# Last attention unit in two query halves, output groups gathered ahead, masked query copies on GpSimd, query tiles 40 rows earlier

## The chip, the cores and the metric

The kernel runs on one core of one Trainium2 chip. The metric is the time of one execution on the device in microseconds (us), as the median of several executions. A profiled execution shows a *span* some 1.7 us shorter, because the span runs only from the first to the last instruction (797.01 us and a span of 795.3 us for the kernel before). Every execution also has a mean granted clock of TensorE, where 1.0 is full speed.

## The reference, cut to what matters

```python
def reference(A_x, A_wqkv, A_wo, B_x, B_w1, B_w3, B_w2):   # x: 1 x 2048 x 512, bf16; 32 heads of 16
    def _A_ref(x, wqkv, wo):
        q, k, v = ...                                       # x @ wqkv, split in heads
        scores = jnp.einsum("bhqd,bhkd->bhqk", q, k) * (Dh ** -0.5)
        p = _softmax(scores, axis=-1)
        o = jnp.einsum("bhqk,bhkd->bhqd", p, v)
        return ... @ wo
    def _B_ref(x, w1, w3, w2):                              # F = 1792
        return (_silu(x @ w1) * (x @ w3)) @ w2
    xn = _layernorm(A_x, axis=-1)
    return A_x + _A_ref(xn, A_wqkv, A_wo) + _B_ref(xn, B_w1, B_w3, B_w2)
```

The work is 2048 x 2048 scores for each of 32 heads. Their exponentials are nearly all that ScalarE does (747.6 of its 772.0 busy us in the kernel before).

## The kernel before

When the kernel is built, a greedy plan in Python lays every instruction in order on its engine, by modelled durations. So a change in one place shifts instructions everywhere.

The attention is 32 *units*: 4 chunks of 512 queries times 8 groups of 4 heads. A unit has 32 *blocks* of scores (128 x 1024), so there are 1024 blocks. ScalarE takes the exponential of most blocks in one instruction. VectorE takes the rest: one instruction reads the scores from PSUM, and four further passes over two blocks at a time run in SBUF. Projections, the feed-forward part and the output projection fill TensorE between the scores.

A pair of units needs a query tile. It is projected by TensorE, scaled by VectorE, and copied twice under a mask (even heads, odd heads):

```python
def tile_QT(qc, i):
    ...
    def emit():
        q = P.op("dve", lambda e: e.tensor_scalar(QT[:, s1, :], bank(bk), QS, None, ALU.mult), ...)
        rel(q)
        q = P.op("dve", lambda e: e.tensor_scalar(QT[:, s0, :], QT[:, s1, :], msk[:, 0:1], None, ALU.mult), ..., lock=True)
        done[("QTm", u0)] = q.end + _LAT
        q = P.op("dve", lambda e: e.tensor_scalar(QT[:, s1, :], QT[:, s1, :], msk[:, 1:2], None, ALU.mult), ..., lock=True)
        done[("QTm", u0 + 1)] = q.end + _LAT
```

A query tile may start once the plan has come to within 60 rows of its unit (a row is half a block, and a unit has RPU = 64 rows). I call this distance the *lead*:

```python
for qc in range(NQC):
    for i in range(NG // 2):
        if qc + i > 0:
            crit.append((max(1, (qc * NG + 2 * i) * RPU - 60), k, tile_QT(qc, i)))
```

The last unit ends in a chain of its own. It copies the products out of PSUM, sums the columns, takes reciprocals, spreads them over the partitions and normalises, all for 512 queries at once:

```python
def last_end(o):
    def copy():      # ACT: U <- PV, 512 columns
    def col_sums():  # PE: 4 matmuls against sell
    def inv():       # DVE: reciprocal; a copy of the sums; l_check (three small operations for the check flag)
    def spread():    # PE: 16 matmuls of the reciprocals against the identity
    def norm_b():    # DVE: onorm <- U * mask * spread; releases ("ON", qc, "B")
```

The last four row tiles of the output add up in a PSUM bank: 14 feed-forward groups of 4 matmuls, and then, in the tail, 5 groups with `wo`:

```python
ats = [og(g, (qc * NP + g) % NON, ("ON", qc, g)) for g in range(NP)]
last_b = [og(NP - 1, ON_B, ("ON", qc, "B"))]
...
gr = {2: ats + last_b, 3: ffn, 4: ats, 5: ffn + res + ats + last_b}[part]
```

Parts 3 and 2 make three of the last row tiles: part 3 goes to SBUF ahead, and part 2 is added to it in the tail. Part 5 is the fourth row tile, made as one sum that stays in its bank.

Of the kernel before, what the change touches and what calls it, by code (L numbers as in the profile page):

```python
# [144 lines left out]
_LAT = 0.06  # L145
# [892 lines left out]
def _plan_fast(nc, ps, flag, A_x, A_wqkv, A_wo, B_w1, B_w3, B_w2, out):  # L1038
# [15 lines left out]
    NR = NU * RPU  # L1054
    NPR = 12
# [12 lines left out]
    D_STOP = 6  # L1068
    NW = 3
    PVQ = 28  # L1070
    R_LAG = 2.5
    A_SOON = 0.7
# [16 lines left out]
    with ctx:  # L1089
# [338 lines left out]

        def tile_KT(i, sc):
# [16 lines left out]
        def tile_QT(qc, i):  # L1446
# [9 lines left out]
            def evac(bk, o, rel):  # L1456
                def emit():
                    q = P.op("dve", lambda e: e.tensor_scalar(QT[:, s1, :], bank(bk), QS, None, ALU.mult),  # L1458
                             reads=[("ps", bk)], writes=[("QT", s1)], dur=d_cost(512), name="evQ")
                    rel(q)  # L1460
                    q = P.op("dve", lambda e: e.tensor_scalar(QT[:, s0, :], QT[:, s1, :], msk[:, 0:1], None, ALU.mult),
                             reads=[("QT", s1), ("msk", 0)], writes=[("QT", s0)], dur=s_cost(512), name="evQ", lock=True)
                    done[("QTm", u0)] = q.end + _LAT
                    q = P.op("dve", lambda e: e.tensor_scalar(QT[:, s1, :], QT[:, s1, :], msk[:, 1:2], None, ALU.mult),
                             reads=[("QT", s1), ("msk", 1)], writes=[("QT", s1)], dur=s_cost(512), name="evQ", lock=True)
                    done[("QTm", u0 + 1)] = q.end + _LAT
                P.post("dve", emit, ready=o.end + _LAT, prio=1)
# [109 lines left out]

        def late():
            return left[NU - 1] <= D_STOP and st["hold_d"] == 0 and pbuf[2] <= P.t or st["pos"] >= NR
        ON_B = (NQC * NP) % NON  # L1580

        def tile_OUT(tg, part):
# [9 lines left out]
            last_b = [og(NP - 1, ON_B, ("ON", qc, "B"))]  # L1592
            res = [(lambda i: ident[:, 32 * i:32 * i + 32], xr[:, ts % 2, :], [("ident",), ("xr", ts % 2)],
                    lambda: have(("xl", tg)))]
            gr = {2: ats + last_b, 3: ffn, 4: ats, 5: ffn + res + ats + last_b}[part]
# [39 lines left out]
            def cond():  # L1635
                if part == 4:
                    return have(("OSUM", tg), ("ON", qc, NP - 1))
                if part == 2:
                    return have(("OSUM", tg)) and (st["pos"] >= NR or late())
                if part == 5 and tg == NT - 1 and not late():  # L1640
                    return False
# [6 lines left out]
                return have(("ON", qc, NP - 1))  # L1648
# [45 lines left out]
        for qc in range(NQC):  # L1694
            for i in range(NG // 2):
                if qc + i > 0:
                    crit.append((max(1, (qc * NG + 2 * i) * RPU - 60), k, tile_QT(qc, i)))
# [35 lines left out]
        taken = [[False] * (RPU // 2) for u in range(NU)]  # L1733
        left = [RPU // 2] * NU
        st["ua"] = 0

        def a_next(avoid=None):
            while st["ua"] < NU and left[st["ua"]] == 0:
                st["ua"] += 1
            if st["ua"] >= NU:  # L1740
# [3 lines left out]
            if avoid is not None and i % 2 == avoid:  # L1744
                for k in range(i + 1, min(i + 6, RPU // 2)):
# [4 lines left out]
        def d_next():  # L1750
# [4 lines left out]
            if left[u] <= D_LEFT and u + 1 < NU:  # L1755
                u += 1
            elif u == NU - 1 and left[u] <= D_STOP:
                return None
            c = [i for i in range(RPU // 2) if not taken[u][i]][:2]
# [8 lines left out]
        def score(b0, name, u, ix):  # L1768
            kt, j0 = ix // 2, ix % 2 * 2
            r0 = u * RPU + 2 * ix  # L1770
            g = u % NG
            g = g // 2
            if not have(("QTm", u), ("KTm", g, kt // 4)):
                return None
            rd = [("QT", u % 4), ("KT", g, kt // 4)]
            mms = []
            for i in range(2):
                j = j0 + i
                mms.append((b0 + i, KT[32 * j:32 * j + 32, g, kt * 128:(kt + 1) * 128],
                            QT[32 * j:32 * j + 32, u % 4, :], 32 * j))  # L1780

            def f(e, mms=tuple(mms)):
                for (b, l_, r_, rp) in mms:
                    ins = e.matmul(bank(b), l_, r_, start=True, stop=True, tile_position=(rp, 0))  # L1784
# [12 lines left out]
        def open_bufs():  # L1797
# [3 lines left out]
            if not st["early"] and idle((4, 5)):  # L1801
# [83 lines left out]
        def try_d():  # L1885
# [19 lines left out]
            if sl is None:  # L1905
                sl = dcur[0] = {"y": None, "p1": 0, "n": 0, "ch": [], "done": 0, "max": 2 if u < NU - 1 or left[u] > D_ONE else 1}
# [95 lines left out]
        def try_pv():  # L2002
            u = pv_unit[0]
            if u >= NU:
# [5 lines left out]
            vi = int(u % NG >= 2)  # L2010
            oldest = P.t
            for j in range(4):
                for tk in tasks[u][j]:
                    if tk[0] <= P.t and have(("V", tk[1], vi)):
# [5 lines left out]
            closed = left[u] == 0 and sum(ntask[u]) == 64 + 4 * nd_unit[u]  # L2020
            if len(pick) < 4 and not closed and P.t - oldest < 2:
                return False
            g = u % NG
            mms, rd, rels = [], [], []
            for j in sorted(pick):
# [4 lines left out]
                stop = left[u] == 0 and npv[u][j] == NT + 2 * ndj[u][j]  # L2030
                w_ = Vaug[:, tk[1], 4 * (g // 2) + j, 0:17] if g % 2 == 0 else Vaug[:, tk[1], 4 * (g // 2) + j, 1:33]
                mms.append((j, w_, tk[2], start, stop))
                rd += [("V", tk[1], vi), tk[3]]
                rels.append(tk[4])

            def f(e, mms=tuple(mms)):
                for (j, v_, p_, s0, s1) in mms:
                    ins = e.matmul(bank(PV)[32 * j:32 * j + (17 if g % 2 == 0 else 32), :], v_, p_, start=s0, stop=s1, tile_position=(0, 32 * j))  # L2038
# [4 lines left out]
            if left[u] == 0 and not any(tasks[u]) and st["n_exp"] >= 0 and \  # L2043
                    sum(ntask[u]) == 64 + 4 * nd_unit[u] and npv[u] == ntask[u]:
# [5 lines left out]
        def unit_end(u, o):  # L2050
            h = u % 2
            qc, pi = divmod(u // 2, NP)
            UK = [("Uc",)] + [("Uo", j_) for j_ in range(4)] if h == 0 else [("Ut",)]
# [40 lines left out]
            def beside_p1():  # L2094
                return st["p1_at"] == P.t

# [21 lines left out]
            if u == NU - 1:  # L2118
                return last_end(o)
            P.post("dve", e0, ready=o.end + _LAT, prio=0, cond=lambda: u < 2 or h == 1 or ("e5", u // 2 - 1) in done)  # L2120

        def last_end(o):
            u = NU - 1
            qc = NQC - 1

            def copy():
                q = P.op("act", lambda e: e.activation(U[:, 1, :], bank(PV), ACTF.Identity), reads=[("ps", PV)],
# [243 lines left out]
```

## Time and profile before

| | before |
|---|---|
| median (range) | 798.34 us (797.80 to 800.65, 4 executions) |
| blocks on ScalarE / VectorE | 798 / 226 |
| last exponential ends | 782.32 us |
| last addition ends (the *tail* is from the last exponential to here) | 790.80 us, so 8.48 us of tail |
| from there to the end (output transfer) | 4.48 us |
| mean TensorE clock of the profiled execution | .996 |

Two groups of the page tell how the exponentials are shared. The columns are line, engine, operation, output and input with their sizes and count; then the total busy us and the mean ns of one; then the idle time ahead of them and what ended most of it:

```profile
L1847 ACT ACTIVATE f_PT<-ps 128x1024 bf16<-128x1024 f32 x798 | 747.6, 1138 | 4.4 <-PE ps L1784 3.7
L1920 DVE TENSOR_SCALAR f_xd<-ps 128x1024 int16<-128x1024 f32 x226 | 275.1, 1217 | 3.0 <-PE ps L1784 2.7
```

ScalarE waits only 4.4 us in all ahead of its 798 blocks. To end sooner it needs fewer blocks, or fewer of these waits, or a shorter tail after the last block.

### The profile page before, as it was taken

How to read it: one execution, taken by the hardware profiler on the slowest of the kernel's cores; microseconds unless marked ns; L12 is line 12 of the kernel's file. 1: busy time of each engine (PE TensorE's matmuls, PEld its weight loads, DVE VectorE, ACT ScalarE, POOL GpSimd, SP SyncE). 2: the span in 40 equal slices, each digit the busy share in tenths (PEclk: the TensorE clock that was granted, in tenths of full speed). 3: DMA queues.
4: the chain of work that ended last, by engine and by line, in shares of the span. 5: the costliest groups of instructions: out<-in, count | busy, mean ns of one | idle time of the engine just before them, and what ended most of it. 6: DMA issues, size and time to landing. Idle time of an engine off the chain costs nothing.

```text
span 795.3 us, 21182 instructions
## 1 busy us (share of the span) xinstructions
PE 750.3 (94%) x9169; PEld 227.6 (29%) x9169; DVE 768.8 (97%) x1039; ACT 772.0 (97%) x872; POOL 38.0 (5%) x60
## 2 busy tenths in 40 slices
PE   8999999999899999999999999998999998999997
PEld 6332222222222222222222222222222222222223
DVE  8899999999999999999999999999999999999993
ACT  5999999999999999999999999999999999999994
POOL 3100201000010000000000000000100000000000
PEclk9999999999999999999999999999999999999989
DMA  7024033331322222233311234322223341332221
GB/s 213 2 23 118 5 35 42 36 34 36 48 35 30 30 36 48 34 48 53 45 17 15 37 47 59 49 33 45 28 22 36 54 60 22 51 35 23 22 15 33
DMA packets 83568, 32.91 MB, mean 41 GB/s; under 512 B 72073, under 2 KB 79753, under 8 KB 83465
## 3 DMA queue, kind: packets, MB, share of 16 engines
q1 hardware_dynamic: 83464, 31.46, 27.6%
q8 instruction: 74, 1.21, 0.6%
q14 instruction: 30, 0.24, 0.1%
HBM read 22.81 MB, written 2.10 MB: 31 GB/s over the span
## 4 chain that ended last, share of the span: by engine, by line
ACT 63%; DVE 23%; PE 12%; issue 1%; DVEq 0%; ACTq 0%
ACT f_PT L1847 60%; DVE f_xd L1920 8%; PE ps L1330 4%; DVE f_xd L1969 4%; PE ps L1784 4%; PE ps L2038 3%; DVE f_xd L1962 2%; ACT f_th L1544 2%; DVE f_xd L1978 2%; DVE f_xd L1984 2%; DVE f_hT L1558 2%; DVE f_t L1548 1%; PE ps L1217 1%; DVE f_U L2056 1%; DVE f_QT L1458 0%
## 5 line engine op out<-in xcount | busy, mean ns | idle before, releaser
L1847 ACT ACTIVATE f_PT<-ps 128x1024 bf16<-128x1024 f32 x798 | 747.6, 1138 | 4.4 <-PE ps L1784 3.7
L1784 PE MATMUL ps<-f_QT,f_KT 32*128 32x512 bf16 x2048 | 310.8, 386 | 26.6 <-ACT f_PT L1847 20.4
L1920 DVE TENSOR_SCALAR f_xd<-ps 128x1024 int16<-128x1024 f32 x226 | 275.1, 1217 | 3.0 <-PE ps L1784 2.7
L2038 PE MATMUL ps<-f_PT,f_Vaug 128*17 128x512 bf16 (+1 forms) x1596 | 210.0, 386 | 3.4 <-DVE f_U L2056 2.2
L2038 PE MATMUL ps<-f_xd,f_Vaug 128*32 128x512 bf16 (+1 forms) x1356 | 182.3, 385 | 3.9 <-DVE f_xd L1969 1.6
L1784 PEld LDWEIGHTS ps<-f_QT,f_KT 32*128 32x128 bf16 x2048 | 79.6, 91 | 323.0 <-ACT f_PT L1847 259.8
L1330 PE MATMUL ps<-f_xnT,f_w 128*32 128x512 bf16 x1792 | 139.9, 384 | 3.0 <-DVE f_t L1548 1.2
L1969 DVE TENSOR_TENSOR f_xd<-f_xd 128x2048 bf16<-128x2048 bf16 x113 | 137.3, 1215 | 0.0
L1962 DVE TENSOR_SCALAR f_xd<-f_xd 128x2048 int16<-128x2048 int16 x113 | 80.5, 713 | 2.7 <-PE ps L2038 1.9
L1984 DVE TENSOR_SCALAR f_xd<-f_xd 128x2048 int16<-128x2048 int16 x113 | 78.0, 690 | 0.0
L1978 DVE TENSOR_SCALAR f_xd<-f_xd 128x2048 int16<-128x2048 int16 x113 | 77.6, 687 | 0.0
L1330 PE MATMUL ps<-f_w,f_hT 128*32 128x512 bf16 x896 | 73.0, 383 | 0.2
L2038 PEld LDWEIGHTS ps<-f_PT,f_Vaug 128*17 128x17 bf16 (+1 forms) x1596 | 51.0, 92 | 63.7 <-issue 45.8
L2038 PEld LDWEIGHTS ps<-f_xd,f_Vaug 128*32 128x32 bf16 (+1 forms) x1356 | 44.5, 92 | 51.3 <-issue 26.9
L2100 POOL TENSOR_TENSOR f_onorm<-f_U,f_R 128x256 bf16<-128x256 f32 x30 | 25.1, 842 | 703.2 <-DMA f_R<-f_Rrow 414.0
L1330 PEld LDWEIGHTS ps<-f_xnT,f_w 128*32 128x32 bf16 x1792 | 36.8, 94 | 62.2 <-issue 51.5
L1544 ACT ACTIVATE f_th<-ps 128x512 f32<-128x512 f32 x56 | 41.0, 733 | 0.0
L1558 DVE SCALAR_TENSOR_TENSOR f_hT<-f_t,ps 128x512 bf16<-128x512 bf16 x56 | 38.0, 679 | 0.4 <-PE ps L1330 0.2
L1548 DVE SCALAR_TENSOR_TENSOR f_t<-f_th,ps 128x512 bf16<-128x512 f32 x56 | 38.0, 678 | 0.3 <-ACT f_th L1544 0.3
L1330 PEld LDWEIGHTS ps<-f_w,f_hT 128*32 128x32 bf16 x896 | 19.3, 95 | 23.7 <-issue 16.3
L2056 DVE COPY f_U<-ps 128x512 f32<-128x512 f32 x31 | 21.2, 685 | 0.4 <-PE ps L2038 0.4
L1330 PE MATMUL ps<-f_wo,f_onorm 128*32 128x512 bf16 x272 | 19.9, 382 | 0.2 <-DVE f_QT L1458 0.2
(81 smaller groups left out, 240.1 us busy)
## 6 DMA issues: line engine op xcount, KB each, us to landing
f_w<-in_B_w_dram SPq DMA_DIRECT2D x112, 128.0 KB, 3.9
f_R<-f_Rrow SPq DMA_DIRECT2D x124, 32.0 KB, 4.1
f_xr<-in_A_x_dram SPq DMA_DIRECT2D x16, 128.0 KB, 2.6
f_U<-f_U SPq DMA_DIRECT2D x60, 32.0 KB, 1.9
f_w<-in_B_w_dram SPq DMA_DIRECT2D x7, 256.0 KB
f_xd<-in_A_x_dram SPq DMA_DIRECT2D x3, 512.0 KB
out_dram<-f_xn_sb SPq DMA_DIRECT2D x12, 128.0 KB
f_xd<-in_A_x_dram SPq DMA_DIRECT2D x2, 256.0 KB
```

The source lines that it names most:

```text
L1330: ins = e.matmul(bank(bk)[32 * i:32 * i + 32, 0:ncols], make_lhsT(i), rhs_ap, start=start, stop=stop, tile_position=(0, 32 * i))
L1544: q = P.op("act", lambda e: e.activation(th[:, ss, :], bank(bk), ACTF.Tanh, scale=0.5), reads=[("ps", bk)], writes=[("th", ss)], dur=a_cos ...
L1548: q2 = P.op("dve", lambda e: e.scalar_tensor_tensor(t1[:, ss, :], th[:, ss, :], 1.0, bank(bk), ALU.add, ALU.mult), reads=[("th", ss), ("ps ...
L1558: q = P.op("dve", lambda e: e.scalar_tensor_tensor(hT[:, fc, :], t1[:, ss, :], 0.5, bank(bk), ALU.mult, ALU.mult), reads=[("t1", ss), ("ps ...
L1784: ins = e.matmul(bank(b), l_, r_, start=True, stop=True, tile_position=(rp, 0))
L1847: q = P.op("act", lambda e: e.activation(PT[:, s_, :], ps[:, b0 * 512:(b0 + 2) * 512], ACTF.Exp, scale=ASC, bias=ABIAS), reads=[("ps", b0) ...
L1920: q = P.op("dve", lambda e: e.tensor_scalar(dsl[:, ys, 1024 * c:1024 * c + 1024], ps[:, b0 * 512:b0 * 512 + 1024], YB, G_LO, ALU.add, ALU. ...
L1962: P.op("dve", lambda e: e.tensor_scalar(dsl[:, NY + m_, 0:n], y, 0x7F, 0x3F00, ALU.bitwise_and, ALU.bitwise_or), reads=YK, writes=[("ds", ...
L1969: q_ = P.op("dve", lambda e: e.tensor_tensor(t_ap.bitcast(BF16), y.bitcast(BF16), t_ap.bitcast(BF16), ALU.mult), reads=YK + [("ds", NY + m ...
L1978: q_ = P.op("dve", lambda e: e.tensor_scalar(g_ap, y, -G_LO, 0.0, ALU.add, ALU.max), reads=YK, writes=[("g", g_, k) for k in range(n // 51 ...
L1984: q_ = P.op("dve", lambda e: e.tensor_scalar(y, y, 0x7F80, None, ALU.bitwise_and), reads=YK, writes=YK, dur=s_cost(n), name="e", lock=True)
L2038: ins = e.matmul(bank(PV)[32 * j:32 * j + (17 if g % 2 == 0 else 32), :], v_, p_, start=s0, stop=s1, tile_position=(0, 32 * j))
```

## The change

The intent is to free VectorE of the masked copies, so that it takes more blocks (the query tiles then have to start 40 rows earlier), and to shorten the tail by normalising half of the last unit before the last exponential and by doing output groups early. The core of the diff (cuts are marked `...`):

```diff
-    D_STOP = 6
+    D_STOP = 4                       # VectorE takes blocks until so many are left
...
-                    q = P.op("dve", lambda e: e.tensor_scalar(QT[:, s0, :], QT[:, s1, :], msk[:, 0:1], None, ALU.mult), ..., lock=True)
-                    ...              # and the second masked copy
+                    P.post("pool", lambda: part(0), ready=q.end + _LAT, prio=1, cond=beside_p1)
+                def part(i):
+                    h, cs = i // 2, slice(256 * (i % 2), 256 * (i % 2) + 256)
+                    d_ = (s0, s1)[h]
+                    q = P.op("pool", lambda e: e.tensor_scalar(QT[:, d_, cs], QT[:, s1, cs], msk[:, h:h + 1], None, ALU.mult),
+                             ..., dur=QP_DUR, extra=[st["p1_op"]])
+                    ...
+                    if i < 3:
+                        P.post("pool", lambda: part(i + 1), ready=q.end + _LAT, prio=1, cond=beside_p1)
...
-                    crit.append((max(1, (qc * NG + 2 * i) * RPU - 60), k, tile_QT(qc, i)))
+                    crit.append((max(1, (qc * NG + 2 * i) * RPU - 100), k, tile_QT(qc, i)))
...
-            gr = {2: ats + last_b, 3: ffn, 4: ats, 5: ffn + res + ats + last_b}[part]
+            na = NP - 2 if ts < 1 else NP - 1
+            gr = {2: ats[na:] + last_b, 3: ffn + ats[:na] if qc == NQC - 1 else ffn, 4: ats,
+                  5: ffn + res + ats + last_b}[part]
...
-                if part == 5 and tg == NT - 1 and not late():
-                    return False
...                                   # scores and value products of the last unit: two key tiles x 256 queries
-        def last_end(o):
+        def last_end(o, hb):          # once for each half of the queries: 256 columns,
+            ...                       # half of the sums, reciprocals, spreading and normalising;
+            ...                       # first half copied by VectorE, second by ScalarE
```

`beside_p1` lets a GpSimd copy start only together with one of VectorE's readings of scores from PSUM.

## The prediction

> **What bounds the kernel now.** I read the busy times first, then the same by stretch of the span, then the chain that ended last, then the timeline around the two places that looked odd. The first view, engine by engine over 795.3 us:
>
> ```profile
> PE 750.3 (94%) x9169; PEld 227.6 (29%) x9169; DVE 768.8 (97%) x1039; ACT 772.0 (97%) x872; POOL 38.0 (5%) x60
> ```
>
> Three engines look full and GpSimd idle. By stretch (columns: stretch, its length, then the busy time of each engine with its instruction count, the TensorE clock, the DMA share and GB/s):
>
> ```profile
> 100.00:400.00 300.00, 285.20 (x3356) 79.92 (x3353) 298.52 (x389) 299.80 (x341) 10.82 (x12) 1.00 0.29 39
> 400.00:740.00 340.00, 323.32 (x3896) 93.17 (x3892) 336.21 (x434) 339.31 (x384) 11.09 (x14) 1.00 0.28 37
> ...
> 778.00:782.40 4.40, 4.40 (x64) 1.43 (x66) 0.31 (x1) 4.32 (x5) 0.00 (x0) 1.00 0.02 4
> 782.40:786.70 4.30, 4.30 (x85) 3.13 (x83) 0.84 (x6) 0.60 (x1) 0.00 (x0) 1.00 0.00 0
> 786.70:791.00 4.30, 3.35 (x61) 1.36 (x60) 3.00 (x6) 0.60 (x1) 0.00 (x0) 1.00 0.23 71
> 791.00:795.30 4.30, 0.00 (x0) 0.00 (x0) 0.00 (x0) 0.00 (x0) 0.00 (x0) 1.00 0.26 77
> ```
>
> There are two regimes. Up to about 782 us ScalarE is the bound (339.31 of 340) with VectorE beside it (336.21): they share the exponentials, 798 blocks of 128x1024 on ScalarE and 226 on VectorE, 1024 in all. Freeing either lets the plan move blocks across. TensorE has some 5% of idle there and waits mostly for ScalarE to release score banks. From 782.4 on, ScalarE and VectorE are nearly idle and TensorE is continuously busy: a serial tail of 13 us, of which the last 4.3 us is only the output transfer. The chain that ended last, by pieces, shows what that tail is (start, duration, what):
>
> ```profile
> 781.05 1.62 PE ps L2038 x26
> ...
> 782.89 1.08 PE ps L1330 x18
> 783.97 0.98 PE ps L2134 x8
> 784.96 0.76 PE ps L1330 x12
> 785.72 0.87 PE ps L2152 x32
> 786.60 0.11 PE ps L2232
> 786.71 3.38 PE ps L1330 x60
> 790.09 0.02 issue
> 790.11 0.69 DVE f_xn_sb L1614
> ```
>
> L2038 is probabilities times V, L2134 the column sums of the last unit and L2152 the spreading of their reciprocals, L1330 here the output projection, L1614 the last addition. The output projection needs 4 row tiles x 5 groups of 4 matmuls = 80 matmuls of f_wo, all of them after 782.8 us. So the tail is bound by TensorE's *work*, not by the latency of its hops.
>
> **What the Trainium skill says.** "SBUF — State Buffer", section "Who interferes with whom": a VectorE instruction with at most one SBUF input, outside the 2-port modes, does not contend with GpSimd, while a 2-port one fully blocks it or is blocked. The change starts each GpSimd copy beside the reading of scores from PSUM (L1920). The trace agrees so far: the GpSimd normalisations, placed by the same rule, run at a median 728 ns (min 725), one in thirty at 1813. "GPSIMD Engine Reference", section "Elementwise — side-by-side cycle accounting": about 2.6 cycles per element for two inputs and 1.8 at best for one, at 1.2 GHz. For 256 elements the first gives 555 ns; the trace's 728 leaves some 173 ns of overhead. "TensorE: Matmul & The Clock Gate", section "Back-to-back issue gap": an isolated warm gap of N/2.4 + 2.5 ns, so 216 ns for 512 columns and 109 for 256. The trace agrees for 512: 60 column-tiled matmuls, four at once, take 3.38 us, which is 225 ns per group of four; no 256-column matmul of the score loop exists in it yet.
>
> **The change, part by part.**
>
> *1. Masked query copies to GpSimd.* Fifteen times, VectorE makes two masked copies:
>
> ```profile
> 68.07 0.35 DVE L1461 TENSOR_SCALAR f_QT<-f_QT,f_msk 128x512 bf16<-128x512 bf16 x1
> ...
> 68.34 0.34 DVE L1464 TENSOR_SCALAR f_QT<-f_QT,f_msk 128x512 bf16<-128x512 bf16 x1
> ```
>
> The records overlap, so I take start-to-start times: 68.07 to 68.34 to 68.60, 0.53 us the pair, 15 x 0.53 = 8.0 us of VectorE freed. A block costs VectorE, by the same start-to-start reading of the loop, 1.13 (L1920) plus half of 1.13 + 3 x 0.60 (the passes over two blocks), 2.6 us; ScalarE needs 0.917 (36.75 us for 40). If x blocks move, ScalarE saves 0.917x and VectorE 8.0 - 2.6x; equal at x = 2.3, which is **2.1 us**. A moved block adds two further value products on TensorE (some 0.2 us a block), which its 5% of idle holds. I keep 1.8 us because the plan is greedy. GpSimd gets 60 copies of 128x256 at an estimated 384 + 173 = 557 ns (skill's 1.8 cycles plus the overhead above), inside the 1.13 us of L1920; 33 us more on an engine that has 757 free.
>
> *2. Query tiles 40 rows earlier.* Four copies now wait for four score readings, some 2.6 to 4 us apart, so a tile is ready 10 to 16 us later. The 40 rows give 40 x 0.375 = 15 us (24 us per unit of 64 rows), so it balances. It also should remove one stall:
>
> ```profile
> 69.00 3.77 ACT L1847 ACTIVATE f_PT<-ps 128x1024 bf16<-128x1024 f32 x4 [1.30 <-PE ps L1784]
> ```
>
> ScalarE sat 1.30 us because the first such query tile was copied only at 67.34 to 68.7, behind the V and K tiles in the single dense bank. From row 28 instead of 68 it would come some 30 us sooner. With VectorE idle 0.75 us at the same place: **1.0 us**.
>
> *3. Last unit in halves.* The exponentials cost the same: 16 blocks of two key tiles x 256 queries for each half instead of 32 of one x 512. Matmuls of the unit double in number at half the length; the streaming time is equal, and ScalarE paces them. The first half's copy, sums (half of 0.98), spread (half of 0.87) and its two row tiles go before the last exponential. VectorE may take blocks to 4 instead of 6 before the end; it was idle from 778.3 to the last exponential at 782.33. Two blocks later at the joint rate (0.68 us a block) is 1.35 us more of VectorE, half a block: **0.35 us**.
>
> *4. Gathering ahead.* Two groups of the first row tile and three of the next two, 8 groups x 0.225 = 1.8 us of TensorE, go into the partial sums before the tail.
>
> *The tail after the last exponential.* Before, 782.33 to 790.80 = 8.47 us. TensorE work there falls by 1.8 us (part 4), 0.93 (half of sums and spread), and the groups of the first two row tiles that find room ahead. Then the latency of the second half's hops decides. From this trace's own durations, halved where the instruction is halved: last value products 0.55; copy on ScalarE 0.38 (0.60 for 512, less 256 x 0.83 ns); to TensorE 0.36; sums 0.50; reciprocal 0.25 with its wait 0.05; spread 0.5 with 0.1; normalise 0.45 with 0.1; last group of two row tiles 0.45 with 0.15; addition 0.69. Sum 4.5 us; with some unavoidable queueing behind other matmuls 5.3. **Saving 3.1 us.** The transfer of 256 KB after it stays at 4.5 us.
>
> Sum: 1.8 + 1.0 + 0.35 + 3.1 = 6.2 us. I take off 0.8 for a plan made anew (each moved tile shifts others, and the end of the D blocks can fall badly), so 5.4 us: 798.4 - 5.4 = **793.0 us**.
>
> **Rivals.** *GpSimd blocks VectorE.* If a copy outlasts L1920, the next 2-port pass waits: 60 copies x 0.3 us would be 18 us of VectorE, 26% of it on the end (0.917 / (0.917 + 2.6)), about 4.7 us given back: near 798 us. Against it: 728 ns of a two-input operation already fits. *Late query tiles.* If the chain of four copies comes late, scores of a pair of units wait; 1 us at each of 15 pairs would give a time above 800. For it: the one-tile stall above; against it: 15 us more of lead, and no other gap of ScalarE that long behind scores in the old trace. *TensorE stays the bound of the tail.* Between 775.4 and 782.4 it is busy without a gap, so work moved ahead may only push the last scores. Then only what moved before 775 counts, some 1.8 to 2.5 us rather than 3.1: 794. *The clock falls.* Around 770 to 773.4 the granted clock is 0.50 in this trace, after a stretch of less busy TensorE; a tail with waits between hops might meet such a stretch and lose 1 to 2 us.
>
> ```profile
> 770.00:773.40 3.40, 3.40 (x24) 0.66 (x22) 3.27 (x5) 3.31 (x4) 0.00 (x0) 0.50 0.67 57
> ```
>
> **Range and chances.** All gains together with no loss come to 792.2, and a luckier plan to 790; the rivals singly give 794 to 798, and the worst of them I hold for unlikely. So 793.0, range 790.0 to 796.5. 2% is 16 us, more than the whole tail: faster 0.01, within 0.98, slower 0.01.
>
> **What would show it.** In the changed trace: L1461 and L1464 gone from VectorE and 60 GpSimd copies of 0.5 to 0.6 us; about two to three more L1920 blocks than 226 and as many fewer ScalarE blocks; no 1.3 us gap of ScalarE near 69 us; the last exponential near 779 instead of 782.33; 5 to 5.5 us from there to the last addition instead of 8.47, with waits between hops where TensorE is now continuously busy; 4.5 us of transfer unchanged. It is wrong if GpSimd copies take over 1.1 us, if ScalarE shows gaps at each pair of units, or if the last exponential does not come sooner.

## The result, and the profile after

The changed kernel takes **788.87 us** (788.16 to 789.84, 4 executions), and the kernel before 798.34 us. The ratio is .9877 (95% interval .9854 to .9900). A ratio here is the mean time of one kernel's runs over that of the other's of the same rounds, so it is not quite the ratio of the medians quoted. The gain is 9.5 us where 5.4 were predicted, and the time lies below the predicted range.

Engine by engine in the changed kernel, then its span by stretches, with the same columns as in the prediction:

```profile
PE 747.1 (95%) x9337; PEld 226.8 (29%) x9337; DVE 764.8 (97%) x1023; ACT 768.5 (98%) x870; POOL 90.7 (12%) x120
```

```profile
100.00:400.00 300.00, 285.01 (x3386) 80.50 (x3386) 296.80 (x378) 298.69 (x340) 34.72 (x40) 0.99 0.30 39
400.00:740.00 340.00, 327.43 (x3908) 92.83 (x3904) 336.08 (x426) 339.96 (x385) 38.18 (x42) 1.00 0.28 37
772.50:777.50 5.00, 5.00 (x118) 3.20 (x116) 3.08 (x9) 4.54 (x5) 0.00 (x0) 1.00 0.00 0
777.50:780.00 2.50, 2.50 (x52) 1.77 (x42) 0.28 (x1) 0.38 (x1) 0.00 (x0) 1.00 0.02 7
780.00:783.40 3.40, 2.57 (x46) 0.96 (x45) 3.14 (x11) 0.60 (x1) 0.00 (x0) 1.00 0.00 0
```

The bound of the main part is as before: ScalarE is busy in 339.96 of 340 us. In the tail the first 2.5 us are still TensorE's, but then VectorE is busy in 3.14 of 3.40 us and TensorE has gaps. The copies and the moved blocks:

```profile
L1866 ACT ACTIVATE f_PT<-ps 128x1024 bf16<-128x1024 f32 x796 | 744.7, 1151 | 3.4 <-PE ps L1803 3.2
L1939 DVE TENSOR_SCALAR f_xd<-ps 128x1024 int16<-128x1024 f32 x228 | 277.2, 1216 | 2.8 <-PE ps L1803 2.5
L1471 POOL TENSOR_SCALAR f_QT<-f_QT,f_msk 128x256 bf16<-128x256 bf16 x60 | 55.3, 922 | 270.5 <-DVE f_xd L1997 112.8
```

Two blocks went from ScalarE to VectorE. A GpSimd copy takes 922 ns, not the 557 I had estimated, and so mostly just fits within VectorE's reading of scores (1216 ns; the median copy starts .25 us after it and ends .045 us before it). From the chain that ended last in the changed kernel (start, duration, what):

```profile
776.35 1.97 PE ps L2066 x58
...
778.65 0.86 PE ps L1332 x12
779.51 0.55 PE ps L2168 x4
...
780.09 0.21 DVE f_Rc L2174
...
780.36 0.18 DVE f_th L1286
...
780.78 0.17 DVE f_accb L1290
780.96 0.59 DVE f_xn_sb L1630
781.55 0.39 DVE f_onorm L2195
...
782.17 0.61 DVE f_xn_sb L1630
```

The second half's value products (L2066) and sums (L2168) are followed in this chain by VectorE alone: the reciprocal, the three check operations (L1286 to L1290), one addition (L1630), the normalisation (L2195), and the last additions. The last exponential ends at 777.46 us and the last addition at 783.37 us, so the tail is 5.91 us instead of 8.48. The transfer takes 4.74 us instead of 4.48.

So 4.9 us of the gain come *before* the last exponential (782.32 to 777.46) and 2.6 in the tail, less .3 in the transfer: 7.2 us between these two profiled executions. The medians are 9.5 us apart, because the profiled execution of the kernel before (797.01 us) was faster than its four timed ones and that of the changed kernel the slowest of its four. My sum had 3.15 us (1.8 + 1.0 + .35) ahead of the last exponential, before the shade of .8. What filled the rest, and why do the executions differ so?

One thing stands out in the timeline of ScalarE. The 1.30 us gap at 69 us is gone: one unbroken row of 50 blocks runs across it (start, duration):

```profile
49.49 46.11 ACT L1866 ACTIVATE f_PT<-ps 128x1024 bf16<-128x1024 f32 x50
```

That was predicted, and the gap is 1.3 us; from start to start ScalarE loses 1.6 us there, because two blocks begin 2.56 us apart that otherwise begin .92 us apart. The other candidate is the clock. The four executions of the changed kernel have mean clocks of .997 to .999. The 45 executions of the kernel before average .9923, and none reaches .997.

### The profile page after: what moved, and what is told of

Read it like the earlier page. It is cut to its first block, busy times and chain, and to the rows that moved or that the text cites. A ratio compares the mean times of both kernels' runs of the same rounds, so it can differ in the third digit from the quotient of the medians.

```text
span 788.1 us, 21640 instructions
## 1 busy us (share of the span) xinstructions
PE 747.1 (95%) x9337; PEld 226.8 (29%) x9337; DVE 764.8 (97%) x1023; ACT 768.5 (98%) x870; POOL 90.7 (12%) x120
## 4 chain that ended last, share of the span: by engine, by line
ACT 82%; PE 11%; DVE 5%; issue 0%; DMA 0%; POOL 0%; DVEq 0%; ACTq 0%
ACT f_PT L1866 78%; PE ps L1332 4%; PE ps L1803 4%; ACT f_th L1555 3%; PE ps L2066 3%; DVE f_xd L1939 1%; DVE f_xd L1988 1%; DVE f_xd L2003 0%; DVE f_xd L1981 0%; DMA f_xd<-in_A_x_dram 0%; DVE f_hT L1569 0%; PE ps L1344 0%; DVE f_t L1559 0%; DVE f_stats L1256 0%; DVE f_xd L1997 0%
## 5 line engine op out<-in xcount | busy, mean ns | idle before, releaser
L1803 PE MATMUL ps<-f_QT,f_KT 32*128 32x512 bf16 (+1 forms) x2112 | 313.6, 378 | 23.3 <-ACT f_PT L1866 17.2
L1939 DVE TENSOR_SCALAR f_xd<-ps 128x1024 int16<-128x1024 f32 x228 | 277.2, 1216 | 2.8 <-PE ps L1803 2.5
L2066 PE MATMUL ps<-f_PT,f_Vaug 128*17 128x512 bf16 (+2 forms) x1640 | 205.1, 378 | 1.1 <-DVE f_U L2086 0.5
L2066 PE MATMUL ps<-f_xd,f_Vaug 128*32 128x512 bf16 (+2 forms) x1416 | 181.9, 377 | 4.6 <-DVE f_U L2086 3.1
L1332 PE MATMUL ps<-f_xnT,f_w 128*32 128x512 bf16 x1792 | 143.1, 386 | 3.7 <-DVE f_t L1559 1.6
L1988 DVE TENSOR_TENSOR f_xd<-f_xd 128x2048 bf16<-128x2048 bf16 (+1 forms) x115 | 139.7, 1215 | 0.0
L1471 POOL TENSOR_SCALAR f_QT<-f_QT,f_msk 128x256 bf16<-128x256 bf16 x60 | 55.3, 922 | 270.5 <-DVE f_xd L1997 112.8
L1981 DVE TENSOR_SCALAR f_xd<-f_xd 128x2048 int16<-128x2048 int16 (+1 forms) x115 | 78.1, 679 | 3.9 <-PE ps L2066 3.1
L2003 DVE TENSOR_SCALAR f_xd<-f_xd 128x2048 int16<-128x2048 int16 (+1 forms) x115 | 78.3, 681 | 0.0
L1997 DVE TENSOR_SCALAR f_xd<-f_xd 128x2048 int16<-128x2048 int16 (+1 forms) x115 | 78.2, 680 | 0.0
L2066 PEld LDWEIGHTS ps<-f_PT,f_Vaug 128*32 128x32 bf16 (+1 forms) x1640 | 51.3, 92 | 58.6 <-issue 45.1
L2066 PEld LDWEIGHTS ps<-f_xd,f_Vaug 128*32 128x32 bf16 (+1 forms) x1416 | 46.1, 92 | 49.0 <-issue 28.5
L1332 PE MATMUL ps<-f_wo,f_onorm 128*32 128x512 bf16 x272 | 22.1, 383 | 0.3 <-DVE f_wkv L1619 0.2
```

What stands on the lines that cost most here:

```text
L1332: ins = e.matmul(bank(bk)[32 * i:32 * i + 32, 0:ncols], make_lhsT(i), rhs_ap, start=start, stop=stop, tile_position=(0, 32 * i))
L1471: q = P.op("pool", lambda e: e.tensor_scalar(QT[:, d_, cs], QT[:, s1, cs], msk[:, h:h + 1], None, ALU.mult), reads=[("QT", s1), ("msk", h) ...
L1803: ins = e.matmul(b, l_, r_, start=True, stop=True, tile_position=(rp, 0))
L1939: q = P.op("dve", lambda e: e.tensor_scalar(dsl[:, ys, 1024 * c:1024 * c + 1024], ps[:, b0 * 512:b0 * 512 + 1024], YB, G_LO, ALU.add, ALU. ...
L1981: P.op("dve", lambda e: e.tensor_scalar(dsl[:, NY + m_, 0:n], y, 0x7F, 0x3F00, ALU.bitwise_and, ALU.bitwise_or), reads=YK, writes=[("ds", ...
L1988: q_ = P.op("dve", lambda e: e.tensor_tensor(t_ap.bitcast(BF16), y.bitcast(BF16), t_ap.bitcast(BF16), ALU.mult), reads=YK + [("ds", NY + m ...
```

## The experiments

Twelve kernels ran beside the kernel before.

**The theories.** Theory C (clock): the kernel before loses time to stretches in which TensorE runs at half speed, like the one around 770 us that stood in the prediction's own view, and the change happens to remove them. Theory W (work): the gain is what the prediction listed, with a larger size of one of the parts, that is waits and VectorE time saved, and the clock plays no part. To tell them apart I took the change to pieces, and in one kernel changed the clock alone.

**A tool for reading them.** Within one kernel the span follows the mean clock (correlation -.86 for the kernel before and -.87 for the changed one). Through all executions of all kernels, some 110, I fitted straight lines with one common slope and a level for each kernel: .44 us for each .001 of clock, with a residual of .55 us (standard deviation). The level at clock 1.0 is an estimate of a kernel's span at full speed. It is given below as *span at full clock*; to be compared only with its like. Two things limit it. The slopes of the single kernels run from .14 to .70 us. And the profiled executions also fall to half clock during the output transfer (in after_again from 784.49 us to the end, in lead_only from 788.04), when TensorE has next to nothing left to do; the mean clock counts that too. So half a microsecond between two estimates means little. A check without the line: executions with a clock of .998 or more have a mean span of 793.7 us in end_filled (4 of them; this is the plan of the kernel before, which itself has none), 791.2 in lead_only (4), 788.5 in masks_only (1) and 787.0 in the changed kernel (7).

| kernel | median, us (before on the same chip) | ratio, 95% interval | mean clock | span at full clock, est. | last exponential | tail |
|---|---|---|---|---|---|---|
| before | 798.34 | | .9923 | 793.2 | 782.32 | 8.48 |
| after | 788.87 (798.34) | .9877 [.9854, .9900] | .9979 | 786.55 | 777.46 | 5.91 |
| before_again | 797.20 (799.27) | .9979 [.9965, .9992] | as before | | 782.21 | 8.63 |
| after_again | 788.92 (799.27) | .9880 [.9861, .9898] | as after | | 776.17 | 5.91 |
| masks_only | 792.39 (799.27) | .9911 [.9895, .9928] | .9952 | 788.3 | 777.65 | 8.57 |
| tail_only | 793.72 (799.27) | .9924 [.9909, .9938] | .9966 | 790.2 | 780.32 | 8.37 |
| lead_only | 793.12 (798.42) | .9936 [.9918, .9953] | .9977 | 790.45 | 777.43 | 9.01 |
| end_filled | 795.52 (798.42) | .9966 [.9949, .9984] | .9983 | 793.3 | 781.77 | 8.47 |
| whole_gather | 791.88 (798.42) | .9920 [.9901, .9939] | .9953 | 788.3 | 777.99 | 7.71 |
| no_gather | 789.53 (798.42) | .9893 [.9874, .9913] | .9986 | 787.4 | 774.54 | 8.44 |
| first_lead | 796.81 (798.80) | .9991 [.9964, 1.0019] | .9938 | 792.9 | 780.61 | 8.64 |
| other_lead | 795.08 (798.80) | .9969 [.9951, .9986] | .9953 | 792.0 | 780.17 | 8.78 |
| copy_512 | 792.36 (798.80) | .9922 [.9908, .9936] | .9970 | 789.0 | 778.64 | 5.91 |
| late_check | 790.72 (798.10) | .9906 [.9891, .9921] | .9970 | 787.2 | 776.45 | 5.96 |

The clocks of before and after are over all their executions (45 and 9), the repeats included. All results were correct.

### before_again and after_again: the two kernels unchanged

No edit. They bound what the same kernel varies by.

> The kernel before, run again, to see how its time varies by execution and with the granted TensorE clock. Theory A (states): the profile of before that the prediction was worked from was its fastest execution (797.0 against a median of 798.3), because half-speed stretches of the clock fall at random; then the clock varies between executions from 0.995 to 0.999, the time follows it by 1 to 2 us, and a half-speed stretch is not always at 768 to 775 us. Theory B (structure): the stretch at 768 to 775 us is made by this kernel's own thin TensorE work there, and it is found again in this profile.

> The changed kernel, run again. Theory A: its half-speed stretches are as frequent as those of before, at other places, and the ratio to before is about 0.990 (the profiles' 788.1 over 795.3) once enough executions are seen. Theory B: no half-speed stretch in its last 30 us, since the last unit's two halves keep TensorE busy, and the ratio stays at 0.988 or below; the last exponential ends at 777 +- 1 us and the last addition 5.5 to 6 us after it.

The half-speed stretch of the kernel before is found again in its second profile (6.8 us from 769.5 us, against 768.0 us in the first), so it seems to belong to that plan (Theory B of the two expectations), while the clock varies from execution to execution (.986 to .996). The kernel before, run as if it were a new one, came out at .9979 of itself, with an interval that leaves out 1. Its five executions happened to have clocks of .993 to .996, its partners .986 to .996. So an interval from a few executions is too narrow here, and a difference of .2% (1.6 us) between two kernels is only to be believed together with its clocks. The changed kernel repeated within .1 us at 788.92; its one slow execution (792.22 us) is also the one with the low clock (.994; the others are at .998 or above).

### masks_only: the masked copies and the lead, without the tail's changes

The kernel before with `tile_QT` of the changed one, and the lead that goes with it (with leads of 60 to 98 rows the plan for GpSimd copies did not come to an end at build time, so the copies could not be tried without the lead; a rebuild with 60, 80, 90 and 98 failed in the same way):

```diff
-                    q = P.op("dve", ... QT[:, s0, :] ... lock=True)      # and the second copy
+                    P.post("pool", lambda: part(0), ready=q.end + _LAT, prio=1, cond=beside_p1)
...                                    # part(i) as in the change
-  crit.append((max(1, (qc * NG + 2 * i) * RPU - 60), k, tile_QT(qc, i)))
+  crit.append((max(1, (qc * NG + 2 * i) * RPU - 100), k, tile_QT(qc, i)))
```

> The kernel before with only the masked copies moved to GpSimd and the query tiles 40 rows earlier; the last unit is whole and the tail is the old one. My prediction priced these at 1.8 + 1.0 = 2.8 us: 795.5. Rival (the masks' gain was mis-sized, the tail's was right): the missing 4 us are here, so 791.5. Expected in the profile either way: 228 or 229 blocks on VectorE, copies of 922 ns, no 1.3 us gap near 69 us, tail of 8.5 us from the last exponential to the last addition.

792.39 us, so 6.9 us below its partner, where prediction parts 1 and 2 together had 2.8. The last exponential came at 777.65 us, as early as in the whole change, while the tail stayed at 8.57. So the surplus over the prediction lies in these two parts, not in the tail.

### tail_only: halves and gathering, with the masked copies on VectorE

The changed kernel with the two VectorE copies put back. The lead stayed at 100.

```diff
-                    P.post("pool", lambda: part(0), ready=q.end + _LAT, prio=1, cond=beside_p1)
+                    q = P.op("dve", ... QT[:, s0, :] ... lock=True)      # and the second copy
```

> The changed kernel with the masked copies back on VectorE (tiles still 40 rows earlier); halves, gathering and new tail kept. My prediction priced the tail with its part of the last unit at 3.1 + 0.35 us and the earlier tiles at 1.0: 794. Rival (the tail or the end of the last unit was mis-sized): 790 to 791. Expected: 226 blocks on VectorE, tail 5.9 us.

793.72 us. The tail, 8.37 us, is hardly shorter than before, although the halves and the gathering are in the kernel. TensorE's timeline says why (start, duration, what):

```profile
781.69 1.12 PE L1332 MATMUL ps<-f_w,f_hT 128*32 128x512 bf16 x14
...
784.86 2.76 PE L1332 MATMUL ps<-f_wo,f_onorm 128*32 128x512 bf16 x48
```

Here the last exponential ends at 780.32 us, and of the last row tile's 56 feed-forward matmuls 28 are still to do after it, and 48 of the 80 matmuls with `wo` as well. The changed kernel has 44 with `wo` left at that point and no feed-forward matmul. So the groups with `wo` were gathered nearly as far as there; it is the feed-forward part of the last row tile that did not find TensorE time before the end. The tail's parts thus did not shorten the tail by themselves; that the other parts make the room for them fits this, but no run shows it by itself. And since this kernel, which also has the new lead, is as fast as 793.7 us, I next took the lead alone.

### lead_only: query tiles 40 rows earlier, nothing else

```diff
-  crit.append((max(1, (qc * NG + 2 * i) * RPU - 60), k, tile_QT(qc, i)))
+  crit.append((max(1, (qc * NG + 2 * i) * RPU - 100), k, tile_QT(qc, i)))
```

> The kernel before with the query tiles 40 rows earlier and nothing else; the copies stay on VectorE. My prediction gave this 1.0 us (the 1.3 us gap of ScalarE near 69 us). Expected 797 to 798 beside 798.3 to 799.3 of before, 226 blocks on VectorE. Rival (much of what masks_only gained was the lead): 795 or less.

793.12 us: **one number in one line takes 5.3 us off**, more than half of the whole change, where the prediction had 1.0. VectorE still makes the copies, and the split of the blocks is still 798 to 226. The gap at 69 us is gone here too:

```profile
48.84 32.35 ACT L1847 ACTIVATE f_PT<-ps 128x1024 bf16<-128x1024 f32 x35
```

But the profiled execution also has no half-speed stretch ahead of the output transfer, and the mean clock is .9977 instead of .9923. At equal clock the estimate is 793.2 to 790.45, so 2.7 us; the remaining 2.6 us is put down to the clock.

### end_filled: the clock alone

The plan of the kernel before, untouched, with eight groups of four dummy matmuls put into TensorE's idle moments between 745 and 775 us of the plan. They write to a bank that is free and is overwritten later, so the result is right. Each waits for the last user of that bank, so an added dependency is the only other difference.

```diff
+        FILL = [(745, 775)]
+        ...
+        for (t0_, o_, m_), (t1_, _, n_) in zip(P.pes, P.pes[1:]):
+            ...                                           # only where TensorE idles and bank 6 is free
+            o_.fn = with_fill(o_.fn, col_groups(lambda i: w2[:, 0, 32 * i:32 * i + 32], xnT[:, 0, 0:512], 512))
```

> The kernel before, its plan unchanged, with eight dummy groups of four matmuls into an idle PSUM bank hung onto matmuls already there between 760 and 773 us; the result stays right. Theory (thin TensorE work halves the clock): both profiles of before have the clock at 0.5 for 6.8 us from 768 or 769.5 us, right after their thinnest 3.4 us (14 matmuls); with 20 or more matmuls in each such window that stretch is gone, ScalarE's gap of 0.6 us there too, the last exponential comes at 780.7 to 781.3 us instead of 782.2, the mean clock rises by 0.003 or more, and the time falls by 1 to 1.5 us. Rival (the clock falls for another reason): the stretch stays and the time is the same or up to 0.5 us longer.

795.52 us against 798.42: the kernel became 2.9 us faster (1.3 to 4.1 by the interval) by *added* TensorE work. Compare the same stretch in the repeat of the kernel before and in this one (stretch, length, busy time with count of TensorE, weight load, VectorE, ScalarE, GpSimd, then clock, DMA share and GB/s). First before_again:

```profile
766.00:769.50 3.50, 2.61 (x22) 0.75 (x22) 3.50 (x4) 3.50 (x5) 0.00 (x0) 1.00 0.54 22
769.50:773.00 3.50, 3.30 (x24) 0.75 (x26) 3.50 (x5) 2.91 (x5) 0.00 (x0) 0.50 0.58 53
```

and end_filled:

```profile
766.00:769.50 3.50, 3.17 (x38) 0.89 (x34) 3.47 (x5) 3.50 (x5) 0.00 (x0) 1.00 0.23 13
769.50:773.00 3.50, 3.33 (x40) 0.83 (x32) 3.50 (x5) 3.50 (x5) 0.00 (x0) 1.00 0.82 33
```

With 22 matmuls in 3.5 us the clock fell to .50 right afterwards, and ScalarE, the bound, lost .59 us of that window (2.91 of 3.50 busy). With 38 matmuls the clock stayed at 1.00 and ScalarE stayed full. The clocks of its six executions are .996 to 1.000. At equal clock the estimate is 793.3 against 793.2, so no change is left over beside the clock's, which also supports the straight line. The profile alone shows less than the medians: from 764 us on ScalarE loses 1.8 us to waits in before_again and .1 here, but this execution met another half-speed stretch at 311 us, so its last exponential comes only .4 us sooner than in before_again (781.77 against 782.21).

The same pattern shows in the other traces. In each I counted the matmuls in windows of 3.4 us. Every half-speed stretch ahead of the output transfer in the profiled executions, 3.4 or 6.8 us long, follows a thin window: in the 3.4 us just before it 16 to 24 matmuls start, where the mean of the kernel before is 39, and TensorE is busy for 2.2 to 2.5 us of them. But a thin window does not bring it each time. The changed kernel has one at 305 us, and its two profiles differ there. The first one:

```profile
305.10:308.50 3.40, 2.32 (x20) 0.75 (x16) 3.40 (x6) 3.40 (x6) 0.00 (x0) 1.00 0.00 0
308.50:311.90 3.40, 3.40 (x30) 0.90 (x28) 2.41 (x5) 2.59 (x3) 0.00 (x0) 0.50 0.15 31
```

and after_again:

```profile
305.10:308.50 3.40, 2.53 (x22) 0.66 (x14) 3.40 (x6) 3.40 (x6) 0.00 (x0) 1.00 0.00 0
308.50:311.90 3.40, 3.19 (x48) 1.13 (x48) 3.40 (x6) 3.40 (x5) 0.00 (x0) 1.00 0.15 30
```

It is the same plan with the same thin window; the clock fell in one execution and not in the other. ScalarE then has a gap of 1.31 us in the first, and its blocks, .3 us ahead of the other's until then, are 1.3 us behind them from there to the end. So this one stretch of 3.4 us cost 1.6 us, and executions of one kernel differ by how many they meet.

### whole_gather: masks and lead with the gathering, the last unit whole

masks_only with the changed kernel's lines in `tile_OUT`:

```diff
-  gr = {2: ats + last_b, 3: ffn, 4: ats, 5: ffn + res + ats + last_b}[part]
+  na = NP - 2 if ts < 1 else NP - 1
+  gr = {2: ats[na:] + last_b, 3: ffn + ats[:na] if qc == NQC - 1 else ffn, 4: ats, 5: ffn + res + ats + last_b}[part]
...
-  if part == 5 and tg == NT - 1 and not late():
-      return False
...
```

> masks_only plus gathering ahead, the last unit still whole. If TensorE's work bounds the old tail, as I predicted, the 8 groups taken out shorten it by 1.8 us: from 8.6 us between last exponential and last addition to 6.8, and the time from 792.4 to 790.6. If the hops' latency bounds it as soon as a little work is gone, it falls by under 1 us and the halves are what pays.

791.88 us, with the tail at 7.71 instead of 8.57 us and the last exponential .3 us later (777.99 against 777.65; the plan gave ScalarE one block more than in masks_only, 797 against 796). The prediction had 1.8 us of TensorE for it; the tail became .9 us shorter, and in all no gain over masks_only is left: the ratios are .9920 and .9911, the estimates at equal clock both 788.3.

### no_gather: the changed kernel with nothing gathered

```diff
-  na = NP - 2 if ts < 1 else NP - 1
+  na = 0
```

> The changed kernel without gathering ahead: all output groups are again left for the tail, the halves stay. If the tail is bound by TensorE's work again, its 5.9 us become 7.7 and the time 790.7. If the halves alone do it, since the first two row tiles can be gathered while the second half's exponentials run, 6.0 to 6.5 and 789.5.

789.53 us, only .6 above the changed kernel (on another chip; the ratios are .9893 and .9880, with overlapping intervals). The tail is 8.44 us, as long as with the unit whole, but the last exponential comes at 774.54 us, 1.6 us *sooner* than in after_again. So gathering does not remove TensorE work; it moves it ahead of the last exponential (80 matmuls with `wo` are left after it here, 44 in after_again), where it is not free. It trades 2.5 us of tail for 1.6 us before it. Of the 1.6 us, some .9 is one block: this plan gave VectorE 229 blocks and ScalarE 795, not 228 and 796. That the gathered work took this block away was not tested apart. And halves without gathering shorten nothing in the tail.

### first_lead and other_lead: which tile's lead it is

The kernel before with the lead of 100 rows only for the first query tile (the one behind the gap at 69 us), or only for the other 14:

```diff
-  crit.append((max(1, (qc * NG + 2 * i) * RPU - 60), k, tile_QT(qc, i)))
+  ... - (100 if qc == 0 and i == 1 else 60)     # first_lead
+  ... - (60 if qc == 0 and i == 1 else 100)     # other_lead
```

> The kernel before with 40 rows of lead for the first query tile alone; the other 14 keep 60. Theory P (the lead acts through the plan that it makes: the one gap near 69 us goes, and the dense work near the end falls otherwise so that TensorE is not thin there): no gap at 69 us, no half-speed stretch near 768 us, mean clock 0.996 or more, 793 to 794.5, nearly all of lead_only's gain from one tile of fifteen. Rival (each of the fifteen tiles was late): only the gap of 1.3 us is won, 797.

> The kernel before with the lead for the other 14 tiles and 60 rows for the first. Theory P: its plan still leaves TensorE thin near the end (18 matmuls in 3.4 us), so the gap at 69 us and a half-speed stretch near 768 to 775 us stay, the clock is 0.992 to 0.995 and the time 796.5 to 798. Rival: 14 of 15 parts of lead_only's gain, 793.5.

Neither theory came out clean. first_lead gave 2.0 us and other_lead 3.7 us by the medians, but by the ratios .7 (not apart from zero, .9964 to 1.0019) and 2.5, together 3.2 of lead_only's 5.1, and at equal clock .3 and 1.2 of 2.7. So only the other 14 tiles have a clear gain, and the two do not add up to the whole. first_lead removed the gap at 69 us, but in its profiled execution a half-speed stretch began at 120.3 us, and ScalarE had a gap of 1.08 us there; its six executions run from 794.26 to 801.44 us with clocks from .999 down to .988 (correlation -.99). other_lead kept the gap (1.30 us at 68.5) and lost the stretch near 768 us, but had one at 311.8. This fits a lead that works on the clock by shifting where TensorE is thinly loaded, while *which* windows become thin is up to the plan; it is not shown. No lead other than 60 and 100 rows was run, so it is also open whether earlier tiles matter or only that the plan fell otherwise.

### copy_512: what a GpSimd copy that does not fit costs

The changed kernel with two copies of 512 columns for each tile instead of four of 256. The plan's modelled duration of a copy was doubled with it (`QP_DUR`, .5 to 1.0), so the plan was made anew as well:

```diff
-  h, cs = i // 2, slice(256 * (i % 2), 256 * (i % 2) + 256)
+  h, cs = i, slice(0, 512)
...
-  if i < 3:
+  if i < 1:
...
```

> The changed kernel with each masked copy as one GpSimd instruction of 512 columns instead of two of 256; the plan has the same end and the same blocks. At 922 ns for 256 columns, 512 should take some 1.7 us, longer than the 1.13 us of the score reading beside it. Theory (GpSimd and VectorE share a port): VectorE's next pass is held for about 0.6 us at each of 30 copies, up to 18 us of VectorE in all, 26% of it on the end: 792 to 793.5, with VectorE passes of over 1 us behind the copies. Rival (the port does not matter): 788.9, the same as the changed kernel.

792.36 us, 3.4 above after_again, with the same 796 to 228 blocks and the same tail; the last exponential is 2.5 us later. Around one copy:

```profile
375.68 1.21 DVE L1938 TENSOR_SCALAR f_xd<-ps 128x1024 int16<-128x1024 f32 x1
375.93 1.56 POOL L1471 TENSOR_SCALAR f_QT<-f_QT,f_msk 128x512 bf16<-128x512 bf16 x1 [3.04 <-DVE f_xd L2002]
376.93 1.11 DVE L1980 TENSOR_SCALAR f_xd<-f_xd 128x2048 int16<-128x2048 int16 x1
```

The copy outlasts the reading of scores (L1938) by .6 us, and VectorE's next pass takes 1.11 us instead of .68. In this kernel 15 passes are stretched like that, by 5.6 us in all; in the changed kernel 6 by 1.8 us, in lead_only 3 by .9, and in the kernel before 8 by 3.5. (Counted are passes over .1 us longer than the median.) So the rival "GpSimd blocks VectorE" is a real mechanism, and the four pieces keep most of it out. It does not explain the whole 2.5 us: 26% of the 3.8 us of added stretching, the prediction's share, is an estimated 1.0 us.

### late_check: the check operations out of the tail's way

I meant to put the three check operations behind the last addition:

```diff
-  done["accb"] = l_check(NU - 1, NU, 2).end + _LAT
+  def check():
+      done["accb"] = l_check(NU - 1, NU, 2).end + _LAT
+  P.post("dve", check, ready=P.t, prio=5, cond=lambda: all(("XE", 4 * qc + i) in done for i in range(4)))
```

> The changed kernel with the last overflow check (three VectorE instructions and what follows them) moved behind the four last additions; plan otherwise unchanged. In the changed kernel's tail VectorE runs from 780.1 us on nearly without a pause, and the check's 0.55 us stand between the last reciprocal and the last normalisation. Theory (the new tail is bound by VectorE's queue): 5.9 us from last exponential to last addition become 5.2 to 5.4 and the time falls by 0.5 us, to 788.3. Rival (the hops through TensorE set it, VectorE has slack): 5.9 us and no change; or the flag, now later, holds the end and the time grows.

A miss, and by my edit. The condition held one addition too early, so the check went just *ahead* of the last addition:

```profile
781.64 0.17 DVE L1290 TENSOR_REDUCE f_accb<-f_th 128x1 bf16<-128x16 f32 x1
781.73 0.68 DVE L1630 TENSOR_TENSOR f_xn_sb<-ps,f_wkv 128x512 bf16<-128x512 f32 x1
```

The tail stayed at 5.96 us, and the flag, now written .2 us after the last addition, came late: 5.73 us from the last addition to the end, against 4.96 in after_again. The median is 1.8 us higher, of which .6 remain at equal clock. Whether VectorE's queue bounds the new tail is left open by this.

## Why the prediction was wrong, point by point

**The sum against the runs.** "By medians" is the step from one kernel to the next along before, lead_only, masks_only, after; "at equal clock" is the same from the estimated spans at full clock.

| step of the prediction | predicted | by medians | at equal clock, est. |
|---|---|---|---|
| 2. query tiles 40 rows earlier | 1.0 | 798.4 - 793.1 = 5.3 | 2.7 |
| 1. masked copies to GpSimd | 1.8 | 793.1 - 792.4 = .7 | 2.1 |
| 3, 4 and the tail | .35 + 3.1 | 792.4 - 788.9 = 3.5 | 1.8 |
| plan made anew | -.8 | | |
| sum | 5.4 | 9.5 | 6.6 |

The medians of lead_only and masks_only are from different chips; by their ratios the step between them is 2.0 us instead of .7. That 6.6 us at equal clock is near the 6.2 us of the prediction's gains before its shade is luck: the lead brought 1.7 us more than predicted, and parts 3 and 4 with the tail 1.7 us less.

**The step that failed** is part 2, "Query tiles 40 rows earlier", with its **1.0 us**. The lead alone measured 5.3 us (3.8 to 6.5 by the interval). I had counted the stall at 69 us, and that was right (the gap of 1.30 us is gone in lead_only). What I left out is that TensorE's clock is not the same in both kernels: I sized every term as if it were. The view with the stretch at .50 stood in my own prediction, but I read it as a risk to the *changed* kernel, not as a loss of the kernel before that a shifted plan could undo. By the estimate, before lost some 3.4 us to such stretches, lead_only 1.0, masks_only 2.1 and after .9, so a gain of 2.4 us falls on the step of the lead, and what the later steps change in it nearly cancels. That the clock alone can be worth this is shown by end_filled (2.9 us with the plan unchanged).

What else the lead did can be read from the starts of ScalarE's blocks, which are .92 us apart where nothing waits. In the two profiles the last exponential comes 4.9 us sooner with the lead (777.43 against 782.32). Of this, 1.1 us are before's half-speed stretch near 770 us; 1.6 are the stall at 69 us; some .65 are waits between 565 and 569 us, after VectorE passes that took 1.2 us instead of .7 beside two GpSimd normalisations:

```profile
562.45 2.40 POOL L2100 TENSOR_TENSOR f_onorm<-f_U,f_R 128x256 bf16<-128x256 f32 x2 [48.99 <-DMA f_R<-f_Rrow]
563.04 1.22 DVE L1962 TENSOR_SCALAR f_xd<-f_xd 128x2048 int16<-128x2048 int16 x1
564.19 1.21 DVE L1984 TENSOR_SCALAR f_xd<-f_xd 128x2048 int16<-128x2048 int16 x1
```

The remaining 1.5 us are many waits under .5 us each. One microsecond is lost again, because lead_only's tail and its transfer are each .5 us longer. The prediction passed over such normalisations: it read "one in thirty at 1813", but in that trace five of thirty took over 1 us (1086 to 1813 ns). Why the lead removed the small waits, and how it thins or fills particular windows, is not settled.

**Parts 1, 3 and 4** held in mechanism. Two blocks moved, as worked out (2.3). The copies' duration was wrong, 922 ns for 557, but below the 1.1 us that I had named as the limit, and so harmless. The size of the tail's part was wrong: with parts 3 and 4 it brought 1.8 us at equal clock, not 3.45. The tail itself came out at 5.91 us for 5.3. VectorE's check operations and an addition stand ahead of the last normalisation, which my chain of hops did not have; that they cost the .6 us is not shown, since late_check moved the check behind that normalisation (though ahead of the last addition) and the tail stayed at 5.96 us. The rival "Late query tiles" did not come true: ScalarE waits 3.4 us in all ahead of its blocks, 4.4 before. The rival "TensorE stays the bound of the tail" was half right. Between no_gather and after_again the last exponential moves back by 1.6 us for 2.5 us of tail (.9 of it one block that changed engines), and in tail_only, without the masked copies on GpSimd, the tail hardly shrinks.

**The shade** of .8 us for "a plan made anew" had the wrong sign. The plan made anew was better, by the estimate mostly because of the clock.

**The range** was drawn from losses more than from gains: "a luckier plan" got 2.2 us, without asking in what respect a plan could be luckier. By the estimate a quarter of the gain lay just there.

## What to carry to other kernels

When a profile shows a stretch at half clock, ask how many matmuls were issued in the few microseconds ahead of it, and count that stretch as a loss which any change of the order may remove or bring; here dummy matmuls alone were worth 2.9 us (1.3 to 4.1). Compare kernels by their clock as well as by their median before giving a difference of a few tenths of a per cent to a cause. And before crediting work "gathered ahead", look whether the engine that does it has room there: here 1.6 of the 2.5 us that it saved were given back ahead of the last exponential.

## What the Trainium skill lacked or had wrong

- "TensorE: Matmul & The Clock Gate", sections "What's actually happening" and "HAM oscillation — how this bites in real kernels": the page gives the rule as no idle gaps of TensorE over about 3.4 us, and in its section "A second HAM failure mode: psum-queue depth-cycling" reports a kernel whose clock swings through frequent short idles. Here the clock fell to .50 with no gap of that length: TensorE was busy in 2.61 of 3.50 us (22 matmuls) ahead of one stretch and in 2.32 of 3.40 us (20 matmuls) ahead of another, and in a second execution of that same place it did not fall. The lengths of the stretches (3.4 and 6.8 us), the value .50 and the variation from run to run agree with the page. What it lacks is how much activity in a window keeps the clock up; these runs do not settle that either.
- The same page, sections "What's actually happening" and "HAM oscillation — how this bites in real kernels", puts the warm-up at the start at under 1% of a span, and the loss by later falls of the clock at 26.7 of 211 us in a kernel that waits for DMA between its matmuls. It has no case as small as this one: an estimated 3.4 of 797 us for the kernel before. Yet the 2.5 us less of it are a quarter of what this change brought, so for an already tuned kernel it is not to be neglected.
- "GPSIMD Engine Reference", section "Elementwise — side-by-side cycle accounting": its best case of 1.8 cycles per element (for a tight loop) led to my 557 ns. A bf16 multiplication by a per-partition scalar measured 922 ns for 256 columns and 1565 ns for 512, so an estimated 2.5 ns for each further element, 3 cycles at the page's 1.2 GHz. The page has no figure for this operation.
- "SBUF — State Buffer", section "Who interferes with whom": agrees. With copies of 256 columns, which mostly end inside the reading from PSUM, 6 passes of VectorE were stretched, with copies of 512, which outlast it, 15, one of them from .68 to 1.11 us (copy_512).
